# One scan per chunk, a head's scale moved to ScalarE, and routing finished once for all tokens

## The chip, the cores and the metric

The program runs on one core of one Trainium2 chip. The metric is the device time of the program in microseconds (us). TensorE is called PE here, VectorE DVE, ScalarE ACT, GpSimd POOL; SP issues most of the transfers, and its queue runs in order.

## The reference

Three layers follow each other, all in float32:

```
# 1. gated linear attention, batch 4, 8 heads, 768 steps, head size 48
state = alpha[t][:, None] * state + outer(k[t], v[t])
y[t]  = q[t] @ state                       # y becomes x: 3072 tokens x 384

# 2. mixture of 8 experts, top 2 by noisy logits
noisy = x @ w_gate + log1p(exp(x @ w_noise)) * noise
w     = softmax over the two largest of noisy
x2    = sum over the two experts of w * (relu(x @ w1[e]) @ w2[e])    # 384 -> 1024 -> 384

# 3. one dense layer
h   = x2 @ w_in                            # 384 -> 2048
out = max(0.01 * h, h) @ w_out
```

## The kernel before

**Attention in 24 units.** A unit is one chunk of 128 steps of one batch, all 8 heads (two heads on 112 partitions, four pairs side by side on the free axis: 512 columns). For a unit DVE makes two running products of the decay: a backward scan `suf` (line 965, 512 columns, from the end of the chunk) and a forward scan `wt` (line 974), in two halves of 256 columns, each of which starts from the reciprocal of the chunk's total decay (line 973), written into the addend of the scan. `kt = k * suf` and `qp = q * wt` follow (lines 988 and 992). POOL multiplies out the chunk's total decay (`tots`, line 978).

PE then turns `kt` (line 1000), forms the scores `kt x qp` (1013), updates the state (1048) and adds the decayed old state (1052), multiplies scores and `v` (1069) and `qp` and the old state (1076), and turns the result into token rows with the gate's logits beside them (1098, `turn_y`). Between them ACT copies results out of PSUM (`kN`, `ar`, `S`, `xt`, `xg`) and POOL masks the scores (`am`, 1022) and decays the state (`sp`, 1039).

**Routing, a tile of four units (512 tokens) at a time.** Some 23 small DVE instructions with three ACT steps and one PE step find the two experts of each token and the row ("slot") that each choice takes in the buffer `x_s`; eight indirect transfers on POOL's queue scatter the rows (line 1191). Six more small instructions per tile form the gather indices (1201) and the two weights (278 to 292).

**Experts and the dense layer, from line 742 on.** Each expert's rows come in two groups (384 and 480 rows); the first groups of experts 0 and 1 hold rows of the first four tiles only, so they can start when those are scattered. Rows are loaded (`xg`, 526), turned (600), split into a high and a low part (`xh` on ACT, 604; `xl` on DVE, 609), and multiplied as three products (742, 781). Weights are split likewise: the high part on ACT (464), the low part by DVE or POOL (468). This part closes the attention's PSUM pools first, so no product of it can start while attention's work is open.

**What sets the order.** A planner (class `Planner`) places every step by estimated durations, due times and the number of buffers of each kind (`Ring`), and the instructions of each engine are then issued in that order; nothing is reordered on the chip. Where it sees PE idle it inserts dummy products (`keep_busy`, line 919). They write into the bank `pC`, whose other part holds the constants and the scan's addend that DVE reads and writes.

PSUM has 8 banks. Before they are used as pC 1, pM 2 (turned keys and states), pS 2, pY 1, pA 2 (token rows, positions, turned expert rows).

## Time and profile before

| | |
|---|---|
| median of 3 runs | 1096.68 us (1092.26 to 1100.07) |
| profiled execution | 1087.71 us, span 1085.9 us |
| PE busy over the span | 1042.8 us (96%) |
| DVE / ACT / POOL busy | 593.7 / 388.2 / 278.5 us |
| transfers | 133.20 MB, mean 123 GB/s |

The span has two very different parts. Up to about 165 us the 24 units run, with all engines at work. From 178.6 us on the products of the experts and the dense layer run on PE almost without a gap. A row of the timeline gives the start, the duration, the engine, the line and what is written from what; in brackets stands the idle time ahead of it and what ended it. A busy PE is not PE at its peak, since products are pipelined.

### The profile page before, as it was taken

The numbers are of one execution on the slowest core, as the hardware profiler recorded it, in microseconds if no ns is written. First come the engines' busy times: TensorE is split into PE (matmuls) and PEld (weight loads), VectorE is DVE, ScalarE is ACT, GpSimd is POOL, SyncE is SP. The second block draws the span as 40 slices with busy tenths as digits, with TensorE's granted clock in tenths as the row PEclk, the third lists the DMA queues.
The fourth block names the chain that finished last, engine by engine and source line by source line (L and its number), as shares of the span: only waits on it lengthen the run. The fifth ranks groups of instructions, "written<-read, shape, count | busy, mean of one in ns | idle before, by whom it ended". The sixth has DMA issues, their size and how long they took to land.

```text
span 1085.9 us, 18172 instructions
## 1 busy us (share of the span) xinstructions
PE 1042.8 (96%) x6839; PEld 999.2 (92%) x6839; DVE 593.7 (55%) x1218; ACT 388.2 (36%) x825; POOL 278.5 (26%) x321
## 2 busy tenths in 40 slices
PE   6999895999999999999999999999999999999997
PEld 5887775999999999999999989899999999999997
DVE  5998997223464565646574233455554545454543
ACT  3755644223354544445453222222222222212211
POOL 3466876200032253424351021410110100000000
PEclk9998997999999999999999999999999999999999
DMA  9667746413464565746567344320101100000000
GB/s 232 203 203 242 237 129 222 157 50 103 148 201 141 179 200 164 226 142 207 180 222 241 116 153 139 92 66 9 59 22 45 34 33 16 22 1 23 1 22 26
DMA packets 78917, 133.20 MB, mean 123 GB/s; under 512 B 8514, under 2 KB 56260, under 8 KB 78820
## 3 DMA queue, kind: packets, MB, share of 16 engines
q1 hardware_dynamic: 72292, 111.89, 33.2%
q0 software_dynamic: 6528, 20.06, 5.7%
q8 instruction: 56, 0.92, 0.4%
q14 instruction: 41, 0.34, 0.1%
HBM read 93.38 MB, written 38.54 MB: 121 GB/s over the span
## 4 chain that ended last, share of the span: by engine, by line
PE 87%; DVE 8%; issue 2%; DMA 1%; ACT 1%; another core or an unknown queue 1%; POOL 0%; DVEq 0%; ACTq 0%; POOLq 0%
PE py L781 39%; PE ph L742 39%; PE pA L600 2%; DVE wt L974 1%; PE pS L1013 1%; DVE suf L965 1%; PE pA L1098 1%; PE pY L1069 1%; PE pC L919 1%; PE pY L1076 1%; DVE kt L988 1%; PE pM L1048 1%; DMA xg<-y_d,gidx 1%; DVE g_z L225 0%
## 5 line engine op out<-in xcount | busy, mean ns | idle before, releaser
L766 DVE SCALAR_TENSOR_TENSOR hl<-ph,hh 128x384 fp32r<-128x384 f32 (+1 forms) x128 | 77.4, 606 | 192.3 <-ACT hh L759 186.1
L752 ACT ACTIVATE hc<-ph 128x384 f32<-128x384 f32 x128 | 63.0, 492 | 300.6 <-PE ph L742 283.3
L755 DVE SCALAR_TENSOR_TENSOR hc<-hc 128x384 f32<-128x384 f32 x128 | 71.4, 558 | 178.2 <-ACT hc L752 178.2
L759 ACT ACTIVATE hh<-ph 128x384 fp32r<-128x384 f32 (+1 forms) x128 | 68.0, 532 | 241.7 <-PE ph L742 236.0
L781 PE MATMUL py<-w2hA,hh 128*128 128x384 f32 (+1 forms) x416 | 141.5, 340 | 1.1 <-issue 1.1
L781 PE MATMUL py<-w2hB,hh 128*128 128x384 f32 (+1 forms) x416 | 141.9, 341 | 0.2 <-issue 0.2
L781 PE MATMUL py<-w2lB,hh 128*128 128x384 f32 (+1 forms) x416 | 140.5, 338 | 0.4 <-issue 0.4
L781 PE MATMUL py<-w2hB,hl 128*128 128x384 f32 (+1 forms) x416 | 140.5, 338 | 0.0
L781 PE MATMUL py<-w2hA,hl 128*128 128x384 f32 (+1 forms) x416 | 140.0, 337 | 0.0
L781 PE MATMUL py<-w2lA,hh 128*128 128x384 f32 (+1 forms) x416 | 139.9, 336 | 0.0
L742 PE MATMUL ph<-xh,w1hA 128*128 128x384 f32 (+1 forms) x384 | 136.4, 355 | 1.4 <-ACT hc L752 0.7
L742 PE MATMUL ph<-xl,w1hA 128*128 128x384 f32 (+1 forms) x384 | 134.3, 350 | 1.0 <-issue 1.0
L742 PE MATMUL ph<-xh,w1hB 128*128 128x384 f32 (+1 forms) x384 | 134.1, 349 | 0.4 <-DVE hl L766 0.4
L742 PE MATMUL ph<-xh,w1lA 128*128 128x384 f32 (+1 forms) x384 | 134.1, 349 | 0.0
L742 PE MATMUL ph<-xl,w1hB 128*128 128x384 f32 (+1 forms) x384 | 133.4, 347 | 0.0
L742 PE MATMUL ph<-xh,w1lB 128*128 128x384 f32 (+1 forms) x384 | 133.3, 347 | 0.0
L804 POOL DMA_INDIRECT xg<-y_d,gidx x48 | 46.5, 968 | 279.6 <-PE pA L600 172.7
L781 PEld LDWEIGHTS py<-w2lA,hh 128*128 128x128 f32 (+1 forms) x416 | 77.3, 186 | 2.2 <-issue 1.2
L781 PEld LDWEIGHTS py<-w2lB,hh 128*128 128x128 f32 (+1 forms) x416 | 77.6, 187 | 1.3 <-issue 0.3
L781 PEld LDWEIGHTS py<-w2hB,hh 128*128 128x128 f32 (+1 forms) x416 | 77.5, 186 | 0.8
L769 DVE TENSOR_TENSOR hl<-hc,hh 128x384 fp32r<-128x384 f32 x128 | 71.4, 558 | 12.3 <-DVE hh L761 0.5
L781 PEld LDWEIGHTS py<-w2hB,hl 128*128 128x128 f32 (+1 forms) x416 | 77.6, 187 | 0.5 <-issue 0.5
(160 smaller groups left out, 1877.3 us busy)
## 6 DMA issues: line engine op xcount, KB each, us to landing
w1s<-in_moe_w_dram SPq DMA_DIRECT2D x32, 384.0 KB
w2s<-in_moe_w_dram SPq DMA_DIRECT2D x32, 384.0 KB
kq<-in_kq_l_dram SPq DMA_DIRECT2D x24, 448.0 KB
nv<-in_v_l_dram SPq DMA_DIRECT2D x24, 256.0 KB
w1s<-in_moe_w_in_dram SPq DMA_DIRECT2D x24, 256.0 KB
w2s<-in_moe_w_out_dram SPq DMA_DIRECT2D x16, 384.0 KB
xg<-x_s SPq DMA_DIRECT2D x32, 180.0 KB
y_d<-ys SPq DMA_DIRECT2D x32, 180.0 KB
```

The source lines that it names most:

```text
L600: nc.tensor.transpose(p[:, d, :n], src[:n, d * 128:(d + 1) * 128], identf[:n, :n])
L742: nc.tensor.matmul(ps[:, :n], a[:, d, fo:fo + 128], x[:, d, :n], start=i == 0, stop=i == len(seq) - 1)
L752: nc.scalar.activation(hc[:, :n], ps[:, :n], AF.Copy)
L755: nc.vector.scalar_tensor_tensor(hc[:, :n], hc[:, :n], 0.01, hc[:, :n], op0=OP.mult, op1=OP.max)
L759: nc.scalar.activation(hh[:, :n], ps[:, :n], AF.Relu)
L766: nc.vector.scalar_tensor_tensor(hl[:, :n], ps[:, :n], 0.0, hh[:, :n].bitcast(FT), op0=OP.max, op1=OP.subtract)
L769: nc.vector.tensor_sub(hl[:, :n], HT[si, "hc"][:, :n], hh[:, :n].bitcast(FT))
L781: nc.tensor.matmul(py[:n, :], h[:, o:o + n], w[:, f % 2, :], start=(f == 0 and i == 0), stop=(f == nf - 1 and i == 2))
L804: nc.gpsimd.indirect_dma_start(out=yg, out_offset=None, in_=y_d[0:rows, :], in_offset=bass.IndirectOffsetOnAxis(ap=gidx[:, c, kk:kk + 1], ...
L919: nc.tensor.matmul(warm, identf, identf, start=True, stop=True)
L965: nc.vector.tensor_tensor_scan(rev(d["suf"][:, :]), rev(d["at"][:, 1:NW + 1]), rev(d1b), 0.0, OP.mult, OP.add)
L974: nc.vector.tensor_tensor_scan(d["wt"][:, i * hc:(i + 1) * hc], d["at"][:, i * hc:(i + 1) * hc], scb[:, 0:hc], 0.0, OP.mult, OP.add)
```

## The change

It touches the attention and the routing; the products of the experts stay as they are.

1. The forward scan is one instruction of 512 columns that starts each pair of heads from 1; the reciprocals go into a tile `rec`, and ACT multiplies `qp` by them, one instruction per pair of heads (four per unit). Both scans write to PSUM (banks pF and pT, one buffer each) where they wrote to SBUF, and `kt` and `qp` read them there. `tots` moves from POOL to DVE.
2. To make room pM and pA go from two buffers to one. In the experts' part a new bank pB alternates with pA.
3. Dummy products go into the bank that the next PE step will write, no longer into pC, which now holds constants only.
4. Gather indices and weights are computed once, for all 24 chunks, after the attention. The copy of the positions out of PSUM is dropped (`sel` reads PSUM).
5. Weight splits that belong to the first expert may no longer go to DVE; the turning of the first group's rows gets the earliest due time; the planner books DVE and POOL as sharing a port for steps marked so; some durations change; routing of tile 3 is issued in runs. Constants of the router are loaded earlier.

```diff
-GAP, FILL, COLD, AHEAD, MARGIN = 0.45, 0.24, 0.45, 0.3, 3.0
+GAP, FILL, COLD, AHEAD, MARGIN = 0.45, 0.24, 0.42, 0.3, 3.0
...
-                    t0 = max(t, self.free[e])
+                    t0 = max(t, self.free[e], self.port if st.port and e in "vg" else 0.0)
...
+FUSED = ((3,),)
+RUN = 10
+TURN = 0.0
...
-        p = XP[key, j] = ps2.tile([128, KD, 128], FT, name="pA")
+        pool, nm = (ps2, "pA") if bank_of[key, j] == "pA" else (pools["P"], "pB")
+        p = XP[key, j] = pool.tile([128, KD, 128], FT, name=nm, bufs=1)
...
-                AUX[i].append([hi, add("vg", dict(v=0.87, g=1.8), lambda en, m=m: split_lo(i, m, en), [hi],
-                                       use=[(fe, R[nm]), (WO[i], R["W"])], phase=phase)])
+                AUX[i].append([hi, add("vg" if phase == 2 else "g", dict(v=0.87, g=1.8) if phase == 2 else 1.8, lambda en="g", m=m: split_lo(i, m, en), [hi],
+                                       use=[(fe, R[nm]), (WO[i], R["W"])], phase=phase, port=True)])
...
-        def keep_busy(n):
+        def keep_busy(area, n):
             for _ in range(n):
-                nc.tensor.matmul(warm, identf, identf, start=True, stop=True)
+                nc.tensor.matmul(area, identf, identf[:, 0:area.shape[1]], start=True, stop=True)
...
-            at=5, kq=4, nv=5, suf=3, wt=3, kt=4, qp=4, pM=2, kN=2, pS=1, pT=1, ar=2, am=2, sp=2, S=2, pY=1, xt=XTB,
-            scr=1, pA=2, xg=XGB, XT=2, W=NA + NB, w1s=2, w2s=2, ph=2, hh=4, hl=4, py=4, ys=3, hc=2, f64=F64B, f64o=2).items()}
+            at=5, kq=4, nv=5, suf=1, wt=1, kt=4, qp=4, pM=1, kN=2, pS=1, pT=1, ar=2, am=2, sp=2, S=2, pY=1, xt=XTB,
+            scr=1, rec=4, pA=1, pB=1, xg=XGB, XT=2, W=NA + NB, w1s=2, w2s=2, ph=2, hh=4, hl=4, py=4, ys=3, hc=2, f64=F64B, f64o=2).items()}
...
             def back():
-                d["suf"] = work.tile([PP, NW], FT, name="suf", bufs=3)
+                d["suf"] = psum.tile([PP, NW], FT, name="pF", bufs=1)
...
-            def forth(i):
-                if i == 0:
-                    d["wt"] = work.tile([PP, NW], FT, name="wt", bufs=3)
-                    d["wv"] = d["wt"].rearrange("p (h c) -> p h c", c=C)
-                nc.vector.reciprocal(d1f[:, :, 0], d["sv"][:, i * HB:(i + 1) * HB, 0])
-                nc.vector.tensor_tensor_scan(d["wt"][:, i * hc:(i + 1) * hc], d["at"][:, i * hc:(i + 1) * hc],
-                                             scb[:, 0:hc], 0.0, OP.mult, OP.add)
+            def forth():
+                d["wt"] = psum.tile([PP, NW], FT, name="pT", bufs=1)
+                nc.vector.tensor_tensor_scan(d["wt"][:, :], d["at"][:, 0:NW], begins, 0.0, OP.mult, OP.add)
+
+            def inverse():
+                d["rec"] = work.tile([PP, HP], FT, name="rec", bufs=4)
+                nc.vector.reciprocal(d["rec"], d["sv"][:, :, 0])
...
-                nc.gpsimd.tensor_mul(tots[:, u, :], d["sv"][:, :, 0], d["at"][:, NW + 1:NW + 1 + HP])
+                nc.vector.tensor_mul(tots[:, u, :], d["sv"][:, :, 0], d["at"][:, NW + 1:NW + 1 + HP])
...
+            def scaled():
+                for p in range(HP):
+                    nc.scalar.activation(d["qp"][:, p], d["qp"][:, p], AF.Copy, scale=d["rec"][:, p:p + 1])
...
+            qq = add("a", 0.72, scaled, [q0], use=[(iv, R["rec"]), (q0, R["qp"])])
...
+        def route_end():
+
+            def gidx_op():
+                nc.vector.scalar_tensor_tensor(gidx.rearrange("p c k -> p k c"), pk_all, float(E * (CAP - 1)), cm_all,
+                                               op0=OP.min, op1=OP.add)
```

**DVE, the start of the program: a unit's instructions.** `at` is the decay, `kq` keys and queries, `pC` the bank with the constants. Before:

```order
L965 SCALAR_TENSOR_TENSOR suf<-at,pC 112x512
L973 RECIPROCAL pC<-suf 112x2
L974 SCALAR_TENSOR_TENSOR wt<-at,pC 112x256
L988 TENSOR_TENSOR kt<-kq,suf 112x512
L973 RECIPROCAL pC<-suf 112x2
L974 SCALAR_TENSOR_TENSOR wt<-at,pC 112x256
```

Now:

```order
L996 SCALAR_TENSOR_TENSOR pT<-at,pC 112x512
L990 SCALAR_TENSOR_TENSOR pF<-at,pC 112x512
L1017 TENSOR_TENSOR qp<-kq,pT 112x512
L1000 RECIPROCAL rec<-pF 112x4
L1013 TENSOR_TENSOR kt<-kq,pF 112x512
L1003 TENSOR_TENSOR tots<-pF,at 112x4
```

The forward scan comes first, and nothing that follows writes into `pC` any more.

**PE, from the last units to the first product of an expert.** `xg` are rows of the first expert's group being turned, `ph` is the expert's first product. Before:

```order
L1098 MATMUL pA<-turn_w,xt 128x112 x4
L1076 MATMUL pY<-qp,sp 48x128 x8
L919 MATMUL pC<-identf 128x128 x4
L1098 MATMUL pA<-turn_w,xt 128x112 x4
L600 MATMUL pA<-identf,xg 128x128 x9
L1162 LDWEIGHTS tri
L1162 MATMUL pA<-ot,tri 128x32
L1163 LDWEIGHTS ones_b
L1163 MATMUL pA<-acc,ones_b 128x32
L538 LDWEIGHTS ones_b
L538 MATMUL pA<-acc,ones_b 128x8
L742 MATMUL ph<-xh,w1hA 128x384
```

Now:

```order
L625 MATMUL pA<-identf,xg 128x128 x3
L1112 MATMUL pY<-am,nv 64x128 x8
L625 MATMUL pA<-identf,xg 128x128 x3
L1119 MATMUL pY<-qp,sp 48x128 x8
L1141 MATMUL pA<-turn_w,xt 128x112 x4
L1213 LDWEIGHTS tri
L1213 MATMUL pA<-ot,tri 128x32
L1214 LDWEIGHTS ones_b
L1214 MATMUL pA<-acc,ones_b 128x32
L1141 MATMUL pA<-turn_w,xt 128x112 x8
L770 MATMUL ph<-xh,w1hA 128x384
```

The three turns of the first group, one of them a few instructions further up, now stand between the last units' steps; behind the attention's last step the product follows at once. The position step shown before (`L1162`) is that of the last tile, which has moved behind the first 18 products; the one shown now is that of the tile before it.

**POOL, the last units.** `am` are masks, `sp` the decayed state, `x_s` a scatter, `w1l`/`w2l` low parts of weights. Before:

```order
L1022 AFFINE_SELECT am<-ar 128x512
L978 TENSOR_TENSOR tots<-suf,at 112x4
L1022 AFFINE_SELECT am<-ar 128x512
L1191 DMA x_s<-xg,si 6913x384
L1039 TENSOR_TENSOR sp<-S,tots 112x192
L1191 DMA x_s<-xg,si 6913x384 x7
L468 TENSOR_TENSOR w1lB<-w1s,w1hB 128x768
L468 TENSOR_TENSOR w2lB<-w2s,w2hB 128x768
```

Now:

```order
L1061 AFFINE_SELECT am<-ar 128x512 x2
L486 TENSOR_TENSOR w1lA<-w1s,w1hA 128x768
L486 TENSOR_TENSOR w2lA<-w2s,w2hA 128x768
L1078 TENSOR_TENSOR sp<-S,tots 112x192
L486 TENSOR_TENSOR w2lA<-w2s,w2hA 128x768
L486 TENSOR_TENSOR w1lA<-w1s,w1hA 128x768
L486 TENSOR_TENSOR w2lA<-w2s,w2hA 128x768
L1239 DMA x_s<-xg,si 6913x384 x6
```

Tile 3's eight scatters, which before reach into the row of seven, now all stand ahead of the last masks; five weight splits have come in behind them.

## Rows read from the trace of the kernel before

**Rows 1.** Stretches: start:end, length, busy PE, weight loads, DVE, ACT, POOL, clock, DMA, GB/s.

```profile
0.00:165.00 165.00, 145.64 (x1792) 124.79 (x1792) 140.99 (x345) 91.19 (x217) 99.62 (x154) 0.95 0.71 209
165.00:178.60 13.60, 2.23 (x14) 1.45 (x13) 10.57 (x26) 6.16 (x13) 9.51 (x8) 0.64 0.85 280
178.60:1086.00 907.40, 894.89 (x5036) 873.00 (x5035) 442.15 (x848) 290.87 (x595) 169.37 (x160) 0.99 0.33 105
...
0.00:30.00 30.00, 20.19 (x203) 18.52 (x205) 17.74 (x32) 11.69 (x27) 9.90 (x34) 0.94 0.90 227
```

**Rows 2.** Timeline of PE at the end of the attention: start, duration, work, idle before.

```profile
151.04 1.16 PE L1013 MATMUL pS<-qp,kt 48*128 48x128 f32 x16
...
163.87 1.15 PE L1098 MATMUL pA<-turn_w,xt 128*128 128x112 f32 x8
166.53 1.02 PE L600 MATMUL pA<-identf,xg 128*128 128x128 f32 x6 [1.51 <-DMA xg<-x_s]
175.38 0.90 PE L600 MATMUL pA<-identf,xg 128*128 128x128 f32 x3 [7.83 <-DVE xl L609]
...
178.56 0.67 PE L742 MATMUL ph<-xh,w1hA 128*128 128x384 f32 x1
```

**Rows 3.** Timeline of DVE: the first units, the last query, a stall.

```profile
5.01 0.17 DVE L973 RECIPROCAL pC<-suf 112x2 f32<-112x2 f32 x1
5.22 0.69 DVE L974 TENSOR_TENSOR_SCAN wt<-at,pC 112x256 f32<-112x256 f32 x1
5.83 0.67 DVE L988 TENSOR_TENSOR kt<-kq,suf 112x512 f32<-112x512 f32 x1
...
12.28 1.22 DVE L965 TENSOR_TENSOR_SCAN suf<-at,pC 112x512 f32<-112x512 f32 x1 [4.98 <-PE pC L919]
13.41 0.67 DVE L992 TENSOR_TENSOR qp<-kq,wt 112x512 f32<-112x512 f32 x1
...
150.11 0.68 DVE L992 TENSOR_TENSOR qp<-kq,wt 112x512 f32<-112x512 f32 x1
...
169.27 4.25 DVE L225 TENSOR_TENSOR g_z<-g_ln,g_um 128x32 f32<-128x32 f32 x1
```

**Rows 4.** Waits of DVE up to 165 us: total us, times, longest.

```profile
DVE pC L973 <- PE pC L919: 4.5, 3, 3.0
```

**Rows 5.** Timeline of PE: the first dummy products.

```profile
7.44 4.80 PE L919 MATMUL pC<-identf 128*128 128x128 f32 x22 [7.44 <-DVE wt L974]
```

**Rows 6.** Groups of DVE and PE up to 179 us: busy us, mean ns.

```profile
L988 DVE TENSOR_TENSOR kt<-kq,suf 112x512 f32<-112x512 f32 x24 | 17.8, 743 | 0.0
...
L289 DVE COPY wts<-g_ws 128x4 f32<-128x4 f32 x5 | 1.3, 264 | 0.2
...
L1201 DVE SCALAR_TENSOR_TENSOR gidx<-pk,g_cm 128x8 uint32<-128x8 f32 x5 | 0.8, 160 | 0.0
...
L919 PE MATMUL pC<-identf 128*128 128x128 f32 x70 | 13.1, 355 | 10.9 <-DVE wt L974 10.9
```

**Rows 7.** Groups of DVE over the span by shape: 384 columns from PSUM and SBUF.

```profile
L769 DVE TENSOR_TENSOR hl<-hc,hh 128x384 fp32r<-128x384 f32 x128 | 71.4, 558 | 12.3 <-DVE hh L761 0.5
L761 DVE CAST hh<-hc 128x384 fp32r<-128x384 f32 x128 | 46.2, 361 | 12.2 <-PE py L781 0.5
...
L609 DVE TENSOR_TENSOR xl<-pA,xh 128x384 fp32r<-128x384 f32 x48 | 25.5, 553 | 17.7 <-ACT xh L604 13.1 <-issue 4.4
...
L789 DVE COPY ys<-py 128x384 f32<-128x384 f32 x7 | 3.9, 558 | 12.6 <-PE py L781 12.6
```

**Rows 8.** Groups of ACT up to 179 us.

```profile
L1057 ACT ACTIVATE S<-pM 112x192 f32<-112x192 f32 x20 | 6.7, 333 | 3.9 <-PE pM L1052 3.1 <-PE pM L1048 0.8
...
L281 ACT ACTIVATE g_wd<-g_wd 128x4 f32<-128x4 f32 x5 | 1.0, 200 | 3.1 <-DVE g_wd L278 3.0
```

**Rows 9.** Timeline of POOL: tile 3's last scatter, and a split beside DVE's stall.

```profile
159.38 1.52 POOL L1191 DMA_INDIRECT x_s<-xg,si  x1 [0.18 <-issue]
...
169.89 1.82 POOL L468 TENSOR_TENSOR w1lB<-w1s,w1hB 128x768 fp32r<-128x768 f32 x1
```

More of the change, by code (lines that the diff above doesn't have):

```diff
@@ L31 @@
 F64B = 2
-XGB = 11
 XTB = 3
@@ L108, in prepare @@
                 st.due = min(st.due, nx.due - nx.longest() - far - st.lat)
+        for st in self.steps:
+            st.due = min(st.due, st.own)
         self.waiting = set(self.steps)
@@ L149, in run @@
             t0, e, st = pick
-            if e == "p" and self.filler and t0 - self.free[e] > self.GAP:
-                self.filler(int((t0 - self.free[e]) / self.FILL if self.free[e] else (t0 - 1.0) / self.COLD))
+            if e == "p" and st.room:
+                gap = t0 - max(self.free[e], self.room_of(st))
+                if gap > self.GAP:
+                    st.room(int(gap / (self.FILL if self.free[e] > 1.5 else self.COLD)))
             st.used = e
@@ L155, in run @@
             self.free[e] = t0 + dur
+            if st.port and e in "vg":
+                self.port = t0 + dur
             st.t0 = t0
@@ L205, in _ @@
         nc.vector.tensor_scalar_add(t3("u"), flat(t["ex"]), 1.0)
+    @op(V)
+    def _():
+        nc.vector.scalar_tensor_tensor(t3("um"), flat(t["u"]), -1.0, flat(t["ex"]), op0=OP.add, op1=OP.subtract)
     @op(A)
@@ L234, in _ @@
         res["oh"] = work.tile([128, 2, n, E], FT, name=tagp + "oh")
-        res["cm"] = work.tile([128, 2, n], FT, name=tagp + "cm")
-        t["m"] = work.tile([128, 2, n], FT, name=tagp + "m")
+        res["cm"], t["m"] = kept or [work.tile([128, 2, n], FT, name=tagp + nm) for nm in ("cm", "m")]
     def pick(k):
@@ L416, in tile_kernel @@
     flag = consts.tile([128, 1], I32)
+    cm_all, m_all, pk_all = (consts.tile([128, 2, NCH], FT, name=nm) for nm in ("cm_all", "m_all", "pk_all"))
     msk = {}
@@ L516, in tile_kernel @@
     ones_e = consts.tile([128, E], FT)
-    scattered, late, taken = [], [], []
+    scattered, late, taken, awaited = [], [], [], []
     def apart(ins, others):
@@ L526, in load_rows @@
         ins = nc.sync.dma_start(xg[:n, :], rows_of(x_s, e, g, j))
-        if g == 0 and e < EARLY:
+        first_rows = g == 0 and e < EARLY
+        if first_rows not in awaited:
+            for other in scattered:
+                if not (first_rows and other in late):
+                    tc.add_manual_dep(ins.ins, other.ins.name, SYNC, reason="the rows of every choice are in their slots")
+            awaited.append(first_rows)
+        if first_rows:
             apart(ins, late)
@@ L1039, in decay @@
                     nc.gpsimd.tensor_mul(d["sp"], prev["S"], tots[:, u, :, None].to_broadcast([PP, HP, D]))
-                dc = add("g", 0.42, decay, [tt], use=[(prev["step"], R["S"])], takes=[R["sp"]])
+                dc = add("g", 0.42, decay, [tt], use=[(prev["step"], R["S"])], takes=[R["sp"]], port=True)
             if not last:
                 def update():
-                    d["pu"] = psum.tile([PP, HP, D], FT, name="pM", bufs=2)
+                    d["pu"] = psum.tile([PP, HP, D], FT, name="pM", bufs=1)
                     for p in range(HP):
@@ L1128, in build_route, with link, links @@
             chain, old = [], list(done_of.get(("chain", gi - 1), []))
-            def link(eng, dur, fn, more=(), **kw):
-                deps = (chain[-1:] or after) + old[len(chain):len(chain) + 1] + list(more)
+            def link(eng, dur, fn, more=(), n=1, **kw):
+                deps = (chain[-1:] or after) + old[len(chain):len(chain) + n] + list(more)
                 if gr[0] < EARLY_TILES:
                     kw.setdefault("due", at_unit(4 * gr[-1] + 5) + RDUE + 0.8 * len(chain))
-                chain.append(add(eng, dur, fn, deps, **kw))
+                kw.setdefault("port", eng == "v")
+                chain.extend([add(eng, dur, fn, deps, **kw)] * n)
                 return chain[-1]
-            def t2(nm):
-                return rt.tile([128, 2, n], FT, name=nm)
-            for eng, fn in gate_top2(nc, rt, lambda: keep["lg"], noise_sb[:, cols, :], desc, n, "g_", keep):
-                link(eng, small, fn)
+            def links(ops):
+                runs = []
+                for eng, fn in ops:
+                    if gr in FUSED and runs and runs[-1][0] == eng and len(runs[-1][1]) < RUN:
+                        runs[-1][1].append(fn)
+                    else:
+                        runs.append((eng, [fn]))
+                for eng, fns in runs:
+                    dur = small if len(fns) == 1 else (small + 0.08) * len(fns)
+                    link(eng, dur, lambda fns=fns: [fn() for fn in fns], n=len(fns))
             def counts():
```

155 lines of the change are left out of this document (85 added, 70 removed).

## The prediction

> **What bounds the kernel now.** I read the busy time by stretches first. From 178.6 us to the end PE is busy for 894.89 of 907.40 us [rows 1], and the change leaves those products as they are; so I look for all of its effect ahead of 178.6 us. There the reader is to see two stretches. Up to 165 us the attention runs, with DVE busy for 140.99 us and PE for 145.64 us; then come 13.6 us in which PE works for 2.23 us [rows 1].
>
> PE's figure is inflated. 13.1 us of it are dummy products [rows 6], so at most 132.5 us were work. DVE comes nearest to its limit: of the 24 us in which it was idle, 4.98 us in one wait and 4.5 us in three were waits for dummy products in the bank that it shares with them [rows 3, 4]. PE's first dummies in turn waited for DVE's scan until 7.44 us and then held the bank for 4.80 us [rows 5].
>
> The timeline of PE shows the hand-over. The last unit's scores start at 151.04 us, the last token rows are turned at 163.87, and the first product of an expert starts at 178.56 us [rows 2]. Between the last two lie a wait of 1.51 us for rows of the first expert, and one of 7.83 us for `xl` on DVE, which stood behind a small routing instruction that took 4.25 us [rows 2, 3]. POOL was splitting weights (1.82 us a piece) beside it [rows 9].
>
> **The change part by part.** I move two points: the start of the last unit's scores (151.04 us), which DVE's work decides, since its last query was formed at 150.11 us [rows 3], and the hand-over from there to the first product (27.5 us).
>
> *Scans.* From start to start a half scan takes 0.61 us and its reciprocal 0.21 us, twice per unit: 1.64 us. A scan of 512 columns takes 1.13 us (12.28 to 13.41) [rows 3]. Now a unit has one such scan, one reciprocal and `tots`. These two have no reader right behind them, so I take 0.1 us each (0.17 us in the row, less the overlap), and bound them at 0.17 each: 1.33 to 1.47 us. The saving is 0.31 us (0.17 at least), in 24 units 7.4 us (4.1 at least); I take 6.
>
> *PSUM operands.* No row shows a scan that writes PSUM, or a product of 512 columns that reads it. The nearest row is `xl`, one input from PSUM and one from SBUF: 553 ns on 384 columns, against 558 ns for `hl` with both in SBUF [rows 7]. So I take nothing. `kt` averages 743 ns where it takes 0.67 us alone [rows 3, 6]; if that excess was contention for SBUF and goes, `kt` and `qp` give back 24 x 2 x 0.07 = 3.4 us. I take 1.5, with ends of 0 and 3.4; the other side of this bound is a rival below.
>
> [...]
>
> *Routing.* Six small instructions per tile leave the path, in lines from 1.3 us down to 0.8 us for five tiles [rows 6]. At about 1 us a tile, and three tiles done ahead of the last unit, that is 3 us. The new order puts some seven instructions of the next tile ahead of the last `kt`: 1.5 us back, at about 0.2 us each.
>
> *The shared bank.* The 9.5 us of waits go, because nothing writes that bank any more. Between zero and all of it could turn into waits for loads, whose engines were 0.90 busy in the first 30 us [rows 1]; I take 8.
>
> Sum: 6 + 1.5 + 3 - 1.5 + 8 = 17 us, so DVE would be ready for the last scores at 134 us.
>
> *ScalarE's part* is new and lies between query and score. Four instructions of 128 columns lie between rows of 200 ns (4 columns) and 333 ns (192 columns) [rows 8]: 0.8 to 1.3 us per unit. ACT is busy for 91.19 of 165 us [rows 1], so 24 x 1.3 = 31 us fit, and only the last unit's share is on the path: 1 us, so 135 us.
>
> *PE as a floor.* Sixteen dummy products now come first. They need nothing from DVE; at 4.80 / 22 = 0.22 us for each of 32 (each is two in the trace) they end near 9 us. Of the 132.5 us of work, about 12 lie behind the last scores, so PE could start those at 9 + 120.5 = 130 us. With DVE at 135 and PE at 130 the two take turns at binding. For that, and for pM and pA with one buffer each, I add 3 us, more as a judgement than as a count: 138 us.
>
> *The hand-over.* PE's own work from the last scores to 165 us was 13.9 us with dummies and waits in it; without them and with the three turns it is 12 us. The rows of the first expert come in time if tile 3's scatters do. The last began at 159.38 us, before a turn at 166.53 [rows 2, 9]; now all eight stand ahead of the last masks, and three units follow tile 3's routing on DVE where one did. What is late next is the single pA bank: each turn waits until ACT and DVE have read the one before (0.55 us on DVE [rows 7], and about as much on ACT). Then there is the decayed state of the last unit, which stands behind two splits of 1.82 us on POOL. I add 3 us: 15 us, with ends of 12 and 20. The 20 is the case that DVE's small instructions again wait behind several splits in a row.
>
> The first product then starts at 138 + 15 = 153 us instead of 178.56: 25.5 us earlier. The profiled execution would take 1087.71 - 25.5 = 1062 us. The median of the runs shown lies 9 us above the profiled execution, so against it I forecast 1096.7 - 25.5 = **1071 us**. What runs later is costed at nothing: fills, the last scatters and the second group's weights lie under the products of the first two groups, and the moved index and weight instructions under the rest, where DVE is half idle (442.15 of 907.40 us). Without that cover the late tiles' scatters would show as PE waits at the third group.
>
> **The rivals.**
>
> *Transfers bind.* Up to 178.6 us some 38 MB moved (165 us at 209 GB/s, 13.6 at 280) [rows 1]. For a product at 153 us, about 36.5 MB are needed by then, 239 GB/s. The first 30 us reached 227 at a share of 0.90. If that is a ceiling, the product starts at 36.5 / 0.227 = 161 us: 1079 us. Against it: 280 GB/s at 0.85 in the later stretch. Chance 0.17.
>
> *PSUM costs more than `xl` shows.* A copy from PSUM takes 558 ns on 384 columns, a cast from SBUF 361 [rows 7]. If `kt` and `qp` each gained those 0.2 us, the front would lose 9.5 us: 1080 us. Against it: two-input instructions show no such gap. Chance 0.08. [...]
>
> *The hand-over stays.* PE stands at the turns, now between the attention's steps, because rows or `xl` come late, and the attention's tail waits behind them. If the whole 13.6 us stretch returns inside the tail and half of the DVE gain is lost to PE waits, the gain is 25.5 - 11.5 - 8.5 = 5.5 us: 1091 us. Chance 0.13.
>
> *Slower: the single pM.* In a unit PE turns keys into pM, ACT copies them out, PE puts update and carry there, ACT copies the state. With one bank the next unit's turn waits for the end of that. I estimate PE's three parts at 0.5 us each, the copies at 0.5 and 0.33 us [rows 8] and the hand-overs at 0.8 us together: 3.1 us. If each of the two copies stands behind 2.2 us of other ACT work (the copies of scores and the four new instructions), the loop is 7.5 us. It decides once it exceeds the 5.9 us per unit of now (23 units from 13.41 to 150.11 us [rows 3]); 24 x 1.6 = 38 us later, less the 9.5 us at the start and the 12.5 us of the hand-over, is 16 us later: 1113 us. Against it: ACT has 74 us to spare. Chance 0.09.
>
> **How the numbers follow.** My forecast's case has 0.53, and reaches from 1061 (the larger saving in each term) to 1081 us; transfers 0.17, PSUM 0.08, hand-over 0.13, pM 0.09. The range from 1058 to 1089 us takes in the first three cases and leaves out the last and most of the hand-over. A change under 1% (11 us) can't be told from none; so faster is 0.78, the same 0.13, slower 0.09.
>
> **What would show it.** In the profile after, the first expert product should start near 153 us, with no PE gap over 4 us between the last token rows and it. DVE should show no wait for PE's dummies in the first 20 us, and `kt` should come down from 743 ns to about 680. It is wrong if PE waits for ACT's `kN` or `S`, if the first turn waits for rows, or if `kt` rises.

## The result, and the profile after

The changed kernel takes 1079.83 us (median of 4 runs, 1078.16 to 1082.96), the kernel before 1094.47 us beside it (4 runs, 1090.24 to 1100.07): a ratio of 0.987 [0.9827, 0.9913], 14.6 us faster. Forecast were 25.5 us. The time lies in the range and on the side that had 0.78, but well above the 1071 us of the likeliest case.

The profiled execution took 1082.96 us (span 1081.2 us) against 1087.71 us (span 1085.9 us). So the traced pair differs by less than 5 us: before's traced execution lies 7 us under the median of its runs, after's 3 us above. What follows is first about this pair.

The stretches of the profile after: start:end, length, then busy time and count of PE, weight loads, DVE, ACT, POOL, the granted clock, the DMA share and GB/s.

```profile
0.00:147.00 147.00, 134.88 (x1644) 114.28 (x1646) 115.85 (x276) 109.86 (x293) 77.85 (x122) 0.93 0.74 219
147.00:161.00 14.00, 11.64 (x132) 9.63 (x130) 5.09 (x12) 6.86 (x13) 12.43 (x10) 0.98 0.58 174
161.00:1081.00 920.00, 898.14 (x5039) 876.27 (x5038) 453.52 (x871) 295.99 (x605) 183.23 (x171) 0.99 0.34 107
```

The 13.6 us in which PE worked for 2.23 us [rows 1] are gone: PE is busy for 11.64 of the 14 us ahead of the products. But the products now fill 920 us where they filled 907.4 [rows 1], with 898.14 us of PE work where there were 894.89. Some 13 us went back behind the point that I moved. PE's own timeline shows both:

```profile
8.09 1.16 PE L1052 MATMUL pS<-qp,kt 48*128 48x128 f32 x16
...
146.15 1.16 PE L1052 MATMUL pS<-qp,kt 48*128 48x128 f32 x16
149.79 0.55 PE L625 MATMUL pA<-identf,xg 128*128 128x128 f32 x3
...
160.88 0.67 PE L770 MATMUL ph<-xh,w1hA 128*128 128x384 f32 x1
...
172.16 0.21 PE L1213 MATMUL pA<-ot,tri 128*128 128x32 bf16 x1 [6.26 <-DVE ot L1195]
...
197.84 0.69 PE L770 MATMUL ph<-xh,w1hB 128*128 128x384 f32 x1 [2.87 <-issue]
```

The first scores start at 8.09 us (18.38 before), the last at 146.15 (151.04 before, [rows 2]), and the first product at 160.88, 17.7 us earlier than 178.56 [rows 2]. The hand-over is 14.7 us. The early turns (149.79) waited for no rows. Then PE waits twice in the products: 6.26 us at a position step, and 2.87 us ahead of the product at 197.84.

Followed through the whole pair, the lead of the kernel after over the one before is:

| at | lead, us |
|---|---|
| scores of unit 0 | 10.3 |
| unit 16 | 12.2 |
| unit 19 | 6.2 |
| unit 20, which the new order places late | -0.9 |
| unit 23 (the last) | 4.9 |
| first copy of a product (`hh`, ACT) | 17.8 |
| 3rd copy, behind the position step | 9.3 |
| 6th | 13.6 |
| 7th, behind a standstill of ACT | 4.6 |
| 9th to about 630 us | 5.2 to 6.4 |
| the last copy, behind the gathers around 680 us | 4.0 |

**The position step.** DVE, in the changed kernel:

```profile
166.92 0.19 DVE L258 TENSOR_REDUCE m_all<-g_z 128x4 f32<-128x32 f32 x1
167.15 4.02 DVE L263 TENSOR_TENSOR g_ca<-g_z,m_all 128x32 f32<-128x32 f32 x1
```

and POOL beside it:

```profile
167.53 1.82 POOL L486 TENSOR_TENSOR w1lB<-w1s,w1hB 128x768 fp32r<-128x768 f32 x1
169.30 1.81 POOL L486 TENSOR_TENSOR w2lB<-w2s,w2hB 128x768 fp32r<-128x768 f32 x1
```

This is the stall of [rows 3] and [rows 9] again, in another place: an instruction of 128 x 32 elements ends at 171.17 us, with the second of two splits that stand back to back. The chain of routing behind it makes `ot`, for which PE waits. I had that case in mind (20 us for the hand-over), but as a delay ahead of the first product. Behind the wait the granted clock is 0.55 from 172.1 to 178 us, and products follow each other at 0.32 us (173.59, 173.91, 174.23), where they do so at 0.17 us from 178.6 us on, at a granted clock of 1.00.

**ACT's standstills.** ACT's timeline around the 7th copy; a bracket gives the idle time and what ended it, and "remote" means that no record of this core explains the end of the wait:

```profile
187.37 0.49 ACT L787 ACTIVATE hh<-ph 128x384 fp32r<-128x384 f32 x1 [0.95 <-PE ph L770]
187.76 0.84 ACT L482 ACTIVATE w2hB<-w2s 128x768 fp32r<-128x768 f32 x1
196.70 0.49 ACT L787 ACTIVATE hh<-ph 128x384 fp32r<-128x384 f32 x1 [8.10 <-remote]
...
684.54 0.49 ACT L780 ACTIVATE hc<-ph 128x384 f32<-128x384 f32 x1 [11.39 <-remote]
```

The last of the nine PE rows that form its product is

```profile
189.91 0.34 PE L770 MATMUL ph<-xh,w1lA 128*128 128x384 f32 x1
```

so ACT, free from 188.60 us on (187.76 + 0.84), began 6.4 us after the end of what it waits for. Beside it POOL issued transfers without a pause:

```profile
188.11 0.98 POOL L1239 DMA_INDIRECT x_s<-xg,si  x1 [0.30 <-issue]
189.39 1.05 POOL L603 DMA_INDIRECT x_s<-xg,freerow  x1 [0.30 <-issue]
...
195.86 0.98 POOL L603 DMA_INDIRECT x_s<-xg,freerow  x1 [0.30 <-issue]
```

The last of fourteen in a row, begun at 178.48 us, ends at 196.84, and ACT goes on at 196.70. The same picture, three or more indirect transfers in a row and ACT late behind PE, stands at 53.0 us (3.5 us late), 79.4 (2.4), 116.2 (3.1) and 684.5 (about 9); in the kernel before at 63.2 us (2.2 us late), at 193 to 200 and at 691 to 693 us. I call these **late signals**. Such a run does not always bring one: at 187.37 us, behind seven of the fourteen, ACT starts 0.27 us after the end of its product. Nothing of the kind was in the prediction.

That ACT waited for its own code instead is unlikely by the trace. It has queues of the kind "instruction", but from 188 to 197 us only the queue of the indirect transfers shows packets:

```profile
q0 software_dynamic: 450, 1.38, 41.0%
```

So three questions went to the chip: do the runs of transfers cause the late signals, and what do they cost; what does the position step cost; and which part of the change made the gain?

### The profile page after: what moved, and what is told of

It is laid out like the page before. It is cut to its first block, busy times and chain, and to the rows that moved or that the text cites. A ratio compares the mean times of both kernels' runs of the same rounds, so it can differ in the third digit from the quotient of the medians.

```text
span 1081.2 us, 18044 instructions
## 1 busy us (share of the span) xinstructions
PE 1044.7 (97%) x6809; PEld 1000.2 (93%) x6809; DVE 574.5 (53%) x1159; ACT 412.7 (38%) x911; POOL 273.5 (25%) x302
## 4 chain that ended last, share of the span: by engine, by line
PE 93%; DVE 2%; issue 1%; ACT 1%; DMA 1%; SPq 0%; POOL 0%; ACTq 0%
PE py L809 40%; PE ph L770 40%; PE pS L1052 3%; PE pA L1141 2%; PE pY L1112 2%; PE pY L1119 2%; PE pA L625 1%; PE pB L625 1%; PE pM L1035 1%; PE pM L1087 1%; PE pM L1091 1%; DMA nv<-in_v_l_dram 1%; DMA xg<-y_d,gidx 1%; DVE g_ca L263 0%; DVE run L1199 0%
## 5 line engine op out<-in xcount | busy, mean ns | idle before, releaser
L770 PEld LDWEIGHTS ph<-xh,w1hA 128*128 128x128 f32 x384 | 73.4, 191 | 6.6 <-issue 3.9
L809 PEld LDWEIGHTS py<-w2hA,hh 128*128 128x128 f32 (+1 forms) x416 | 77.7, 187 | 0.8
```

The source lines that it names most:

```text
L770: nc.tensor.matmul(ps[:, :n], a[:, d, fo:fo + 128], x[:, d, :n], start=i == 0, stop=i == len(seq) - 1)
L809: nc.tensor.matmul(py[:n, :], h[:, o:o + n], w[:, f % 2, :], start=(f == 0 and i == 0), stop=(f == nf - 1 and i == 2))
```

## The experiments

The first four ran on one chip (kernel before 1095.31 us, 17 runs); the pair above, whose kernel before takes 1094.47 us, is counted with them. The next four and the last four ran on two other chips, where the kernel before takes 1080.61 us (23 runs) and 1080.14 us (11 runs). Kernels of different chips are compared by their ratio to the kernel before on the same chip. The expectations of runs 5 to 8 still count from the times of the first chip.

**1. Pauses between the transfers.** A short memset follows each of the 102 indirect transfers on POOL, in the functions that scatter, fill and gather:

```diff
+            nc.gpsimd.memset(zrow, 0.0)
```

> The changed kernel with one more POOL instruction (a memset of 1 x 384, about 0.41 us) behind each of POOL's 102 indirect transfers, so that they no longer follow each other directly. Theory A (late signals): in the changed kernel ACT stands still although PE has finished its work, each time while POOL issues several indirect transfers in a row (2.8 us at 50 us, 2.2 us at 114 us, 8.1 us at 189 us, 11.4 us at 673 us). If it is the direct succession, these waits go: the first expert product starts at 153 to 157 us instead of 160.9, the wait at 189 us falls under 3 us, and the median falls to 1064 to 1073 us. Theory B: the waits come from the transfers themselves or from the engines' own chains; the pauses then only make the last scatters and fills later (14 x 0.4 = 5.6 us): 1080 to 1087 us.

Measured: 1070.99 us (6 runs, 1068.11 to 1076.53), ratio 0.9791 [0.9759, 0.9824], 8.8 us faster than the changed kernel had been. The seventh copy, at 196.70 us in the changed kernel, starts at 182.79, and ACT's list of waits has no line with "remote" any more. Its two longest lines (total, times, longest) are

```profile
ACT hc L781 <- PE ph L771: 279.5, 121, 3.2
ACT hh L788 <- PE ph L771: 227.8, 113, 4.4
```

where those of the changed kernel include

```profile
ACT hc L780 <- remote: 11.4, 1, 11.4
ACT hh L787 <- remote: 9.9, 2, 8.1
```

More work on POOL made the kernel faster. What follows: back-to-back indirect transfers go with the standstills, and breaking them up removes the long ones. Shorter ones stay in the attention. Beside four transfers with pauses between them PE's scores end at 50.60 us (49.44 + 1.16), and ACT copies them 2.2 us later:

```profile
49.44 1.16 PE L1054 MATMUL pS<-qp,kt 48*128 48x128 f32 x16
52.79 0.60 ACT L1058 ACTIVATE ar<-pS 128x512 f32<-128x512 f32 x1 [2.62 <-PE pA L1143]
```

The last scores start at 142.12 us instead of 146.15. How a run of transfers holds up a signal from PE to ACT is not shown.

The pauses moved something else too. POOL reaches its two splits only at 167.26 us, when DVE is through with the routing, and PE's wait at the position step is 2.82 us in place of 6.26. So the 8.8 us are not the price of late signals alone.

**2. The splits of the second expert on DVE alone**, so that no two splits on POOL stand beside the routing:

```diff
-                AUX[i].append([hi, add("vg" if phase == 2 else "g", dict(v=0.87, g=1.8) if phase == 2 else 1.8, lambda en="g", m=m: split_lo(i, m, en), [hi],
+                AUX[i].append([hi, add("v" if e == 1 else "vg" if phase == 2 else "g", 0.87 if e == 1 else dict(v=0.87, g=1.8) if phase == 2 else 1.8, lambda en="v" if e == 1 else "g", m=m: split_lo(i, m, en), [hi],
```

> The changed kernel with the weight splits of the second expert allowed on DVE only, so that POOL runs no split of 1.82 us beside DVE's routing of the last tile. Theory A: PE's wait of 6.26 us at 165.9 us, ahead of the last tile's position step, comes from one DVE instruction of 0.19 us that took 4.02 us beside two POOL splits; it falls to 2 to 3 us, the last tile's scatters start some 3 us earlier, and the median falls by 2 to 4 us, to 1076 to 1078 us. Rival: what follows (the run of scatters and fills, the ACT standstill at 189 us) sets the time of the next products whatever happened before it, and the median stays at 1079 to 1081 us.

Measured: 1077.50 us (4 runs, 1073.92 to 1086.26), ratio 0.9829 [0.979, 0.9867]: 2.3 us less than the changed kernel, with intervals that overlap. In its trace PE's wait at the position step is 3.0 us where it was 6.26, but that execution (1086.26 us) also holds two standstills of ACT, of 8.2 and 8.8 us, beside the scatters and fills. For the time this is inconclusive; that the splits lengthen the wait, it supports. So do runs 1 and 9, which keep the splits: there POOL reaches them after the routing, and the wait is 2.82 and 2.15 us.

**3. The kernel before once more**, unchanged, for a trace nearer its median than the 1087.71 us that I had read.

> The kernel before once more, for a second trace of it. The traced execution took 1087.71 us, the others 1090 to 1100. If the spread comes from waits whose length differs between executions, the second trace, at about 1094 us, has its extra 6 us in some three or four places where ACT or PE stand still beside a run of POOL's indirect transfers; if it comes from the start (loads, dummies) its first scores or its first expert product (178.56 us) are later by as much and the products take the same 907 us.

Measured: 1096.05 us, span 1094.2 us. It too has late signals, and one of them ahead of the first product:

```profile
172.80 0.49 ACT L1102 ACTIVATE xg<-pA 128x384 f32<-128x384 f32 x1 [5.27 <-remote]
```

beside six scatters from 165.58 to 172.94 us, such as

```profile
169.42 0.97 POOL L1191 DMA_INDIRECT x_s<-xg,si  x1 [0.31 <-issue]
```

Its first product starts at 184.29 us instead of 178.56. So the kernel before pays for late signals too, in one execution more than in another, and the one that I forecast from had none ahead of its products that cost much.

**4. The kernel before without dummy products**, for what the shared bank cost:

```diff
-            if e == "p" and self.filler and t0 - self.free[e] > self.GAP:
+            if False and e == "p" and self.filler and t0 - self.free[e] > self.GAP:
```

> The kernel before without any dummy products (the planner's filler is off); everything else is unchanged. Theory A: the 9.5 us in which DVE waited for dummies in the shared bank go, the first scores start at 9 to 11 us instead of 18.4, and the median falls by 6 to 9 us, to 1086 to 1089 us. Rival: without dummies the granted clock starts at half, PE takes twice as long in the first units, and nothing is won: 1092 to 1097 us.

Measured: 1091.26 us (10 runs), ratio 0.9959 [0.9934, 0.9984], 4.1 us faster. The first scores start at 9.24 us instead of 18.38, but the third unit's at 26.33 against 26.56: within three units the lead is used up.

```profile
9.24 2.08 PE L1013 MATMUL pS<-qp,kt 48*128 48x128 f32 x16 [1.43 <-DVE qp L992]
...
17.67 2.55 PE L1069 MATMUL pY<-am,nv 128*64 128x128 f32 x16 [4.39 <-POOL am L1022]
```

Sixteen products take 2.08 us where they take 1.16 in the row at 8.09 of the changed kernel, whose granted clock is 1.00 from 0 to 16 us. Without dummies PE starts slow, and POOL, still at the constants, is late with `am`. The changed kernel keeps the 10 us at the start: it has dummies that nobody waits for, and earlier constants. My term (8 of 9.5 us) was priced on the bank alone; freeing the bank without the rest did not keep the gain.

**5. The same pauses in the kernel before.**

```diff
+            nc.gpsimd.memset(zrow, 0.0)
```

> The kernel before with the same POOL memset behind each indirect transfer as in the spaced variant of the changed kernel (1071 us). It separates the change from the late signals. Theory A: the kernel before loses less to them in the attention (1.5 to 2 us at two places against 2.5 to 3.5 us at three or four places in the changed kernel) and about as much later; pauses bring it 3 to 8 us, to 1087 to 1092 us, and the change itself is worth 16 to 21 us between the two spaced kernels. Rival: the kernel before gains as much as the changed one (9 us, to 1086 us) and the change is worth 15 us with or without pauses. Second rival: the pauses cost the kernel before time, because its scatters bind: 1098 us or more.

Measured: 1088.10 us (6 runs), ratio 1.0072 [1.0053, 1.009]: 7.5 us slower, its first product at 185.44 us. The time itself falls where it was expected, but by accident: this chip's kernel before takes 1080.61 us, not 1095. Every kernel traced on this chip has pauses, so none of its traces shows what happens without them. But its kernel before takes as long as the next chip's (1080.61 and 1080.14 us), and there, in three kernels without pauses (runs 9, 11 and 12), ACT never stands late behind a run of transfers by over 0.7 us. So the pauses probably had nothing to remove here, and cost what they cost. The question that this run was to answer, whether the kernel before loses as much to late signals as the changed one, it leaves open.

**6. Scans to SBUF.** The changed kernel with pauses, and only the place of the two scans undone; the order of instructions stays:

```diff
-                d["suf"] = psum.tile([PP, NW], FT, name="pF", bufs=1)
+                d["suf"] = work.tile([PP, NW], FT, name="suf", bufs=1)
...
-                d["wt"] = psum.tile([PP, NW], FT, name="pT", bufs=1)
+                d["wt"] = work.tile([PP, NW], FT, name="wt", bufs=1)
```

> The spaced changed kernel (1071 us) with the two scans written to SBUF, one buffer each, in place of PSUM; the order of the instructions is the same. Theory A (the forecast's): operands in PSUM cost DVE nothing; kt stays within 0.66 to 0.72 us, the scans at 1.2 us, and the median stays within 1068 to 1074 us. Rival 1: PSUM operands cost DVE a fixed time; kt and the scans get shorter by 0.05 us or more each and the last scores come 4 to 6 us earlier: 1064 to 1067 us. Rival 2: contention in SBUF; kt rises to 0.74 us and the last scores come 2 to 4 us later: 1073 to 1076 us.

Measured: 1078.17 us (10 runs), ratio 0.9977 [0.9964, 0.9989], against 0.9818 with the scans in PSUM (run 10): about 17 us of the gain. On PE its last scores and first product are

```profile
153.05 2.08 PE L1054 MATMUL pS<-qp,kt 48*128 48x128 f32 x16
...
170.96 0.67 PE L771 MATMUL ph<-xh,w1hA 128*128 128x384 f32 x1
```

and in run 10, with PSUM, 131.62 and

```profile
146.08 0.42 PE L771 MATMUL ph<-xh,w1hA 128*128 128x384 f32 x1
```

The direction is that of the second rival, contention in SBUF, but it is larger than its 2 to 5 us. DVE's instructions show why. Shortest, median and longest of the 24, in ns, with SBUF:

```profile
L1015 DVE TENSOR_TENSOR kt<-kq,suf x24: 654/663/2041, 6.5 to 147.6; 112x512 f32<-112x512 f32 x24
L1019 DVE TENSOR_TENSOR qp<-kq,wt x24: 659/666/3261, 5.8 to 145.7; 112x512 f32<-112x512 f32 x24
L1005 DVE TENSOR_TENSOR tots<-suf,at x24: 148/154/1868, 7.1 to 148.3; 112x4 f32<-112x4 f32 x24
```

With PSUM:

```profile
L1015 DVE TENSOR_TENSOR kt<-kq,pF x24: 649/655/681, 6.4 to 127.7; 112x512 f32<-112x512 f32 x24
L1019 DVE TENSOR_TENSOR qp<-kq,pT x24: 670/673/689, 5.7 to 125.2; 112x512 f32<-112x512 f32 x24
L1005 DVE TENSOR_TENSOR tots<-pF,at x24: 132/152/153, 6.9 to 128.4; 112x4 f32<-112x4 f32 x24
```

The medians are alike; the longest are not. The worst case with SBUF, on DVE and on POOL beside it:

```profile
103.75 3.26 DVE L1019 TENSOR_TENSOR qp<-kq,wt 112x512 f32<-112x512 f32 x1
```

```profile
103.48 1.81 POOL L486 TENSOR_TENSOR w2lA<-w2s,w2hA 128x768 fp32r<-128x768 f32 x1
105.24 1.23 POOL L1063 TENSOR_SCALAR_AFFINE_SELECT am<-ar 128x512 f32<-128x512 f32 x2
```

`qp` starts 0.27 us behind POOL's split and ends after POOL's next work too: it is held. With one input in PSUM none of the 48 instructions of `kt` and `qp` is longer than 689 ns, and none of `tots` longer than 153. So DVE's instruction was held beside POOL's work with both inputs in SBUF (3261 ns at the longest), and none was with one in PSUM (689 ns). What holds it is not shown. Summed over all of DVE's instructions up to 160 us, the excess over the shortest of each kind (line and shape) is 31.5 us with SBUF and 17.8 us with PSUM. Most of the difference lies in the three instructions whose operand moved: `tots` 4.5, `qp` 4.2 and `kt` 3.1 us with SBUF, against 0.4, 0.1 and 0.3 us with PSUM. PE, which waits longer, has a granted clock of 0.92 instead of 0.98 up to 147 us.

**7. One of four scalings.** The changed kernel with pauses; three of the four query scalings per unit are left out, so that part of the computation is missing.

```diff
-                for p in range(HP):
-                    nc.scalar.activation(d["qp"][:, p], d["qp"][:, p], AF.Copy, scale=d["rec"][:, p:p + 1])
+                nc.scalar.activation(d["qp"][:, 0], d["qp"][:, 0], AF.Copy, scale=d["rec"][:, 0:1])
```

> The spaced changed kernel (1071 us) in which ACT scales one pair of heads per unit instead of four: three of four factors of the queries are left out, so the output is another one. It takes 3 x 0.29 us of ACT out of each unit (21 us in all, 0.9 us of them behind the last query). Theory A: ACT's new work is hidden but for the last unit and for waits of the scores on it; the last scores start 1 to 3 us earlier and the median is 1068 to 1070 us. Rival: ACT has become the engine that binds the attention; the last scores start 8 us or more earlier and the median is 1059 to 1064 us.

Measured: 1059.32 us (4 runs), ratio 0.9823 [0.9798, 0.9848], the same as 0.9818 with all four (run 10, on the next chip). ScalarE's new part is off the path: last scores at 132.75 us against 131.62. The time is the rival's, but only because this chip is faster than the one that the expectation counts from.

**8. A second pM bank**, in the kernel of run 6, where the banks of the scans are free:

```diff
-                d["pk"] = psum.tile([128, HP, PP], FT, name="pM", bufs=1)
+                d["pk"] = psum.tile([128, HP, PP], FT, name="pM", bufs=2)
...
-                    d["pu"] = psum.tile([PP, HP, D], FT, name="pM", bufs=1)
+                    d["pu"] = psum.tile([PP, HP, D], FT, name="pM", bufs=2)
```

> The spaced changed kernel (1071 us) with both scans in SBUF and one of the two freed PSUM banks given to pM, which has two buffers again; the order of the instructions changes with it. Theory A: a single pM costs little (PE waited 0.2 us for ACT's copy of the state in front of a turn of keys up to 148 us), so the median stays within 1068 to 1074 us. Rival: the single bank ties PE's steps to ACT's copies in the order that the planner writes; with two the last scores start 3 to 8 us earlier: 1063 to 1068 us.

Measured: 1084.08 us (10 runs), ratio 1.0035 [1.0022, 1.0048], 6 us slower than run 6 with one bank. The planner, told of two banks, makes another order, so the run does not test the bank alone. In that order the last scores come 7 us earlier than in run 6 (146.10 against 153.05 us), as the rival had it. But PE then stands at a position step ahead of the last token rows, and the first product is 3.8 us later:

```profile
146.10 1.16 PE L1054 MATMUL pS<-qp,kt 48*128 48x128 f32 x16
154.48 0.19 PE L1215 MATMUL pA<-ot,tri 128*128 128x32 bf16 x1 [7.21 <-DVE ot L1197]
...
174.78 0.67 PE L771 MATMUL ph<-xh,w1hA 128*128 128x384 f32 x1
```

A second bank with its own order wins nothing here; what it would win in the order of run 6 stays open.

**9. The changed kernel once more**, unchanged, on the third chip, whose traces show no late signals.

> The changed kernel again, beside the kernel before on the same chip, for a second trace of it. On one chip the kernel before took 1095 us, on another 1081 us, and no trace from the second shows a late signal of PE. Theory A: the change moves the runs of indirect transfers without lengthening them, and what they cost depends on the chip: where the kernel before takes 1093 to 1098 us the changed one takes 1078 to 1083 us again; where the kernel before takes 1079 to 1083 us the late signals are missing in both, and the changed kernel takes 1060 to 1068 us. Rival: the change wins nothing but the waits that only a chip with late signals has; where the kernel before takes 1081 us, the changed one takes 1076 to 1084 us.

Measured: 1057.59 us (5 runs, 1054.40 to 1061.83) against 1080.14: ratio 0.9805 [0.9787, 0.9822], 22.5 us faster. The trace (1054.40 us, span 1052.7 us):

```profile
132.49 1.16 PE L1052 MATMUL pS<-qp,kt 48*128 48x128 f32 x16
...
146.93 0.42 PE L770 MATMUL ph<-xh,w1hA 128*128 128x384 f32 x1
...
153.69 0.21 PE L1213 MATMUL pA<-ot,tri 128*128 128x32 bf16 x1 [2.15 <-DVE ot L1195]
```

and its stretches:

```profile
0.00:147.00 147.00, 137.42 (x1772) 117.31 (x1772) 122.57 (x288) 115.59 (x306) 89.11 (x130) 0.98 0.81 235
153.60:160.80 7.20, 6.56 (x22) 6.01 (x23) 2.94 (x11) 1.33 (x2) 6.46 (x5) 0.53 0.74 258
```

The last scores come at 132.49 us where they came at 146.15, and the hand-over is 14.4 us. The position step holds PE for 2.15 us, and the clock is granted at 0.53 for some 7 us behind it. Here POOL reaches the two splits only when DVE has written `ot`:

```profile
153.40 0.23 DVE L1195 TENSOR_TENSOR ot<-g_oh 128x32 bf16<-128x32 f32 x1
154.84 1.85 POOL L486 TENSOR_TENSOR w1lB<-w1s,w1hB 128x768 fp32r<-128x768 f32 x1
```

**10. The pauses on the same chip**: the kernel of run 1, unchanged.

> The spaced changed kernel again, as the reference for the variants with scans in SBUF (1078 us), with two buffers for pM (1084 us) and with one scaling per unit (1059 us), which ran on another chip than it. Theory A: where PE's signals come late (the kernel before at 1095 us), the pauses win 6 to 11 us against the changed kernel; where they don't (1081 us), the pauses only delay the scatters, and it takes 0 to 8 us more than the changed kernel. Rival: the pauses help in another way, and it is faster than the changed kernel on either chip.

Measured: 1058.84 us (4 runs), ratio 0.9818 [0.9792, 0.9843], the same as run 9 within the intervals. Where there are no late signals, pauses neither help nor cost in the changed kernel. So the 8.8 us of run 1 belong to what only the first chip shows: the late signals, and with them the position step that met POOL's splits there. In the paused kernel the last scores come at 131.62 us here and at 142.12 there, a difference that pauses did not remove.

**11. Half of the scalings on DVE** instead of ACT:

```diff
-                for p in range(HP):
+                for p in range(HB):
                     nc.scalar.activation(d["qp"][:, p], d["qp"][:, p], AF.Copy, scale=d["rec"][:, p:p + 1])
+            def scaled_v():
+                for p in range(HB, HP):
+                    nc.vector.tensor_scalar(d["qp"][:, p], d["qp"][:, p], d["rec"][:, p:p + 1], None, op0=OP.mult)
...
-            qq = add("a", 0.72, scaled, [q0], use=[(iv, R["rec"]), (q0, R["qp"])])
+            qq = add("a", 0.6, scaled, [q0], use=[(iv, R["rec"]), (q0, R["qp"])])
+            qv = add("v", 0.35, scaled_v, [q0], use=[(iv, R["rec"]), (q0, R["qp"])])
```

> The changed kernel with the scaling of a unit's queries shared: two pairs of heads on ACT, two on DVE (a tensor_scalar of 112 x 128 each). Theory A: ACT's four scalings per unit, costed in the forecast at 1 us in all, are what the attention waits for; half of them on DVE bring the last scores 3 to 8 us earlier, and the median falls 3 to 8 us below that of the changed kernel on the same chip. Rival: DVE and ACT bind in turn, DVE's two more instructions (0.2 us each, 24 units) stand on the same chain, and the median stays within 2 us of the changed kernel's, or rises.

Measured: 1066.24 us (6 runs), ratio 0.9878 [0.9854, 0.9902], 8.7 us slower than run 9; last scores at 144.67 us. The group on DVE (busy us, mean ns) costs more than I had put in:

```profile
L1025 DVE TENSOR_SCALAR qp<-qp,rec 112x128 f32<-112x128 f32 x48 | 15.6, 366 | 0.0
```

With 15.6 us more on DVE the last scores come 12.2 us later, while taking three quarters of the scalings off ACT (run 7) gains nothing. This points to DVE as what still binds the attention. It is no clean test, since the planner also makes another order.

**12. The kernel before on this chip**, for a trace to set beside run 9.

> A third trace of the kernel before, on the same chip as the changed kernel's second one. Theory A: at 1093 us or more it shows ACT waiting for signals of PE that stand beside three or more indirect transfers in a row, at 1083 us or less none over 1 us; the time from the first expert product to the end is 907 us in the one case and 900 to 903 us in the other. Rival: the 14 us between the chips lie in the transfers at the start or in the clock of PE, and the waits are the same.

Measured: 1082.11 us, span 1080.4 us, no late signal.

```profile
150.54 1.16 PE L1013 MATMUL pS<-qp,kt 48*128 48x128 f32 x16
...
178.29 0.67 PE L742 MATMUL ph<-xh,w1hA 128*128 128x384 f32 x1
```

Up to the first product it equals the execution that I had read (151.04 and 178.56, [rows 2]). Its products then end 902.1 us later, in the other 907.3. Against it the lead of run 9 is 18.1 us at the last scores, 31.4 at the first product, 26.3 behind the position step and 27.7 at the end. The medians differ by 22.5 us: run 9's traced execution is the fastest of its five, and this one lies 2 us above its median.

By the ratios no version beat the changed kernel on the second and third chip. On the chip with late signals the one with pauses does: 1070.99 against 1079.83 us.

## Why the prediction was right or wrong

**Last scores, 151 to 138 us.** Without late signals they start at 132.5 us, better than forecast; with them at 146.15. The sum came out near, but not by its terms.

- *PSUM operands* is the term that was mis-sized: 1.5 us, bounded at 3.4; run 6 shows about 17 to 19 us (17 by the ratios, 19.3 by the two times). That is what the place is worth in the changed kernel. I priced the mean excess of `kt` and `qp` in the kernel before, and that part was right (743 to 663 ns, and `qp` to 675 ns; I wrote about 680). Three things were missing. In the changed kernel with its scans in SBUF the two exceed their shortest by 7.3 us, where the old means gave 3.3, so the old rows were no measure of what PSUM saves there. `tots`, now on DVE and with the same operand, adds 4.5 us, and the sum had nothing for it. And a hold on DVE delays each instruction behind it, PE's scores with them, and the granted clock of PE up to 147 us is 0.92 where it is 0.98 with PSUM: the last scores of run 6 come 21.4 us later than those of run 10, while DVE's excess differs by some 14 us. How the rest comes about is not shown. The upper end of 3.4 us was no bound: it allowed no gain beyond the two instructions' own lengths. The rival "PSUM costs more" is refuted: the medians are 655 against 663 ns for `kt` and 673 against 666 for `qp`, from PSUM and from SBUF.
- *Scans, routing, shared bank* (6, 1.5 net and 8 us) weren't tried one by one in the changed kernel. All of the change but the place of the scans is worth 2.4 us in run 6, and up to 7.5 us more if the pauses cost there what they cost the kernel before (run 5; in the changed kernel they cost nothing). That is less than the sum of these terms and the hand-over. Run 4 shows how a gain of 9 us at the first unit is given back by the third. How much each of the three is worth stays open. So where the total came near the forecast, that was luck: one term gave far more than its 1.5 us, and the others together far less than theirs.
- *ScalarE's part*, 1 us, was right (run 7: nothing measurable). One scaling takes 396 ns, longer than the rows that I took it from, but they overlap, and the four of a unit take about 1.27 us, the upper end of my 0.8 to 1.3:

```profile
48.99 1.27 ACT L1021 ACTIVATE qp<-qp,rec 112x128 f32<-112x128 f32 x4
```


**Hand-over, 27.5 to 15 us.** Right: 14.7 and 14.4 us.

**First product 25.5 us earlier.** 17.7 in the first pair, 31.4 without late signals.

**Later work costed at nothing.** This is the step that failed. I wrote that fills, scatters and the moved routing lie under the products. The products give back 13 us in the first pair, 3.7 us without late signals. Two things do it. The routing of tile 3, moved behind the first products, makes PE wait for `ot` (6.26 or 2.15 us), and behind the wait the granted clock is 0.55 or 0.53 for 6 or 7 us: the 20 us case of the hand-over, in another place. And the scatters and fills now stand beside ACT's copies, where ACT stood still for 8.10 us. The standstill of 11.39 us at the gathers is not of the change's making: they were not moved, and the kernel before stands still there too (5.45 us, ahead of 692.72 us). That late signals go with runs of transfers was seen in none of the rows that I had read, though the trace before holds them at 63, 193 and 691 us; I had not looked past 178.6 us because PE was busy there.

**From 25.5 to 14.6 us.** On the third chip the median gain is 22.5 us, near the forecast. On the first chip pauses give back 8.8 us of the missing 10.9 (run 1). That sum holds late signals and a part of the wait at the position step, which fell by 3.4 us in run 1's trace; no run separates the two.

**The rivals.** *Transfers bind*: refuted; run 9 moved 235 GB/s up to its first product at 146.93, and the ceiling of 227 was none. Its number, 1079, is the one measured, by another cause. *The hand-over stays*: no. *The single pM*: no; PE waited 0.2 us for `S` in all of the attention, and the kernel got faster, not slower.

**What would show it.** DVE had no wait for dummies in the first 20 us, and `kt` fell, as forecast. The product near 153 us failed in both directions (160.88 and 146.93).

## What to carry to other kernels

Where one engine's instruction is held beside another's work, as `qp` on DVE beside POOL's in run 6, price an operand's move to another memory by every instruction that reads it and by the chain behind the held one, not by one instruction's mean. Look at the longest of a group (3261 ns at a median of 666) before its average. And when work is moved under another stage, ask which short instruction there has a reader waiting, and whether it will stand behind a long one.

## What the runs showed that I had not expected

- Three or more indirect transfers back to back on POOL go with signals from PE that reach ACT 1 to 9 us late, on one chip. On the third chip none behind a run of transfers is above 0.7 us, and the kernel before is 15 us faster there (1080 against 1095 us); the second chip is as fast, but was traced with pauses only. A memset between transfers removes the long ones; some of about 2 us remain. Why it depends on the chip stays open.
- A multiplication of 112 x 128 elements by a value per partition, SBUF to SBUF, takes 366 ns on DVE and 396 ns on ACT: DVE, otherwise bound, had nothing to win from it.
- In run 9 PE's clock was granted in full (1.00) from 147 to 153 us, in which PE was busy for 3.88 of 6 us. A wait of 2.15 us, which ended at 153.69 us, reaches into that stretch, and the clock over the 7.2 us behind it was 0.53. The wait of 6.26 us at the same step in the first trace was followed by 5.9 us at 0.55: the low clock behind the shorter wait did not last less long.
